# An opening ordered by a list schedule, value's halves swapped and 1/rms by tokens in a linear-attention and SwiGLU kernel

## The chip, the cores and the metric

The kernel runs on one core of a Trainium2 chip. A core has five engines with an instruction queue each: TensorE (PE, with its weight loads as PEld), VectorE (DVE), ScalarE (ACT), GpSimd (POOL) and SyncE (SP, which issues transfers here). The metric is the device time of one execution in microseconds (us), lower is better.

## The reference

The input has 4 batches, 8 heads, 768 steps and 48 dimensions a head. First a linear attention with decay, then a feed-forward block on its output, 3072 tokens of 384 features:

```python
for t in range(S):
    kt, vt, rt = (k[:, :, t], v[:, :, t], r[:, :, t])
    cur = np.einsum('bhd,bhe->bhde', u[None] * kt, vt)
    y[:, :, t] = np.einsum('bhd,bhde->bhe', rt, state + cur)
    state = w[None, :, :, None] * state + np.einsum('bhd,bhe->bhde', kt, vt)
...
rms = np.sqrt(np.mean(x * x, axis=-1, keepdims=True) + 1e-06)
xn = x / rms * rms_g
g = xn @ w_gate
silu = g * (1.0 / (1.0 + np.exp(-g)))
val = xn @ w_val
return (silu * val @ w_out).astype(np.float32)
```

The three feed-forward weights (384 x 1536 twice, 1536 x 384) arrive as 64-bit floats, the rest as 32-bit floats.

## The kernel before

The 768 steps are cut into 12 chunks of 64; a chunk holds all 4 batches, so 256 tokens. Everything is done in 32-bit floats; a product in the code is two passes on TensorE.

**Mixing a chunk.** `mix(s, what)` (line 501) gives a chunk's steps in the order of a string of letters. R and K multiply r and k by powers of the decay (`decay_r`, `decay_k`; tiles ME, MO and CH, the profile's `chan`). 1, 2 and 3 form the bonus u·r·k by tokens (TOK, du), and d writes it as a diagonal into ME and MO (`diagonal`, line 316: on VectorE for chunk 0 and in part for chunk 1, else eight small ScalarE instructions a call and side). a are the scores, 32 small matmuls a half (`pa`), and m copies them under a mask into ME and MO. y are the outputs, 48 matmuls a half (`py`), whose squares (sq) and copies scaled by rms_g (yT) ScalarE keeps. q adds the squares of the three feature blocks on VectorE, r sums them over features with a matrix of ones on TensorE (`pm`, every row the same) and takes the root, n takes the reciprocal of 128 x 256 elements and scales: xa from the upper 64 rows of yT, xb from the lower 64, each copied to the other 64 rows by ScalarE. h weights the keys (KH), u makes the states (`pu`), which ScalarE copies into VS for the next chunk. The next chunk's transfers are issued by the step that frees their tile.

**The feed-forward block.** `gate_val(s, nn)` makes gate and value of 128 features for a chunk, 6 matmuls with xa and the half wa of the weights, 6 with xb and wb; the two halves of the array's rows hold gate and value. A Silu on ScalarE and a product on VectorE give h. `add_cell(q, s)` multiplies three h with a quarter of w_out (`po`) and adds to the chunk's sum.

**Weights.** Each of the 24 pieces of 128 x 576 64-bit floats is loaded by SP into a raw tile and rounded to 32 bits by `round_piece` (line 189): one instruction on ScalarE (ulp), two on VectorE (bits), one sum on POOL (line 209). `rounded(count)` forces rounding up to what a product needs.

**Opening and blocks.** The first two chunks take the plain path in the *opening*, lines 526 to 559 and 673 to 677: calls of `gate_val`, `add_cell`, `mix`, `rounding` and `warm` in an order written out by hand. The opening has 24 `gate_val`, 8 `add_cell` and the mixing of chunks 0 to 3. `warm(n)` gives n matmuls of ones that keep TensorE at work. From line 679 on, the *blocks* treat two chunks at a time, with seven products in place of eight for each pair of feature groups (sums of weights s1 to s4, sums of tokens t1 to t4); they mix the two chunks after them in the same time. Each engine runs in program order: `InOrder` (line 81, recorded as line 89) fixes that for PE, DVE and ACT.

Of the kernel before, what the change touches and what calls it, by code (L numbers as in the profile page):

```python
# [89 lines left out]

@with_exitstack
def fast(ctx, tc, chan, tok, vpad, w, u, wka, wkb, wot, g_cols, out, bad):
# [8 lines left out]
    pe, dve, act = (InOrder(tc, engine) for engine in (nc.tensor, nc.vector, nc.scalar))  # L102
    wide = wka.dtype == I64
    PIECE = NQ * CC * P
    CUT = PIECE // 2
# [11 lines left out]
    raws = loading.enter_context(tc.tile_pool(name="raws", bufs=6))  # L117
# [5 lines left out]
    wraw = c_tile([P, HP], "wraw")  # L123
    dve.memset(wraw, 1.0)
    eps = c_tile([P, 1], "eps")
    dve.memset(eps, EPS)
    w_v = w.rearrange("(a e) d -> e d a", e=2)
    with nc.allow_non_contiguous_dma(reason="w, one column for each pair of heads"):
        for z in range(2):
            act.dma_start(out=wraw[64 * z : 64 * z + D, :], in_=w_v[z])  # L130
# [8 lines left out]
    def load_chan(s):  # L139
        for z in range(2):  # L140
            nc.sync.dma_start(out=CH[64 * z : 64 * z + D], in_=chan[s, z])

    def load_tok(s):
        nc.sync.dma_start(out=TOK, in_=tok[s])

    def load_v(s):
        nc.sync.dma_start(out=VS[64:128, 0], in_=vpad[s, 64:128])
        nc.sync.dma_start(out=VS[0:64, 1], in_=vpad[s, 0:64])

    utab = c_tile([P, HP, D], "utab")  # L150
    gcol = c_tile([P, CC], "gcol")
    for z in range(2):

        (dve, nc.gpsimd)[z].memset(CH[64 * z + 32 : 64 * z + 64], 0.0)
    load_tok(0)
    load_chan(0)
    for z in range(2):
        src = bass.AP(tensor=u.tensor, offset=u.offset + z * D, ap=[[0, 64], [2 * D, HP], [1, D]])
        act.dma_start(out=utab[64 - 64 * z : 128 - 64 * z], in_=src)
    act.dma_start(out=gcol, in_=g_cols)  # L160

    spare = c_tile([P, 1], "spare")
# [6 lines left out]
    pieces = [
        (dst[i], src[i], k) for i in range(WQ) for dst, src in ((wa, wka), (wb, wkb), (wo, wot)) for k in range(2)  # L170
    ]
    PER_Q = len(pieces) // WQ
    queue, staged, state = deque(pieces), deque(), {"done": 0}

    def stage():
        if not queue:
            return
        dst, src, k = queue.popleft()
        cols = slice(k * CUT, (k + 1) * CUT)
        flat = dst.rearrange("p a b -> p (a b)")[:, cols]  # L180
        if not wide:
            nc.sync.dma_start(out=flat, in_=src[:, cols])
            staged.append((flat, None))
            return
        raw = raws.tile([P, CUT], I64, name=f"raw_{len(queue)}", tag="raw")
        nc.sync.dma_start(out=raw, in_=src[:, cols])
        staged.append((flat, raw))

    def round_piece():

        if not staged:
            return
        dst, raw = staged.popleft()
        if raw is not None:
            words = raw.bitcast(I32).rearrange("p (n z) -> p n z", z=2)
            hi, lo = words[:, :, 1], words[:, :, 0].bitcast(U32)
            n = state["done"]
            bits = raws.tile([P, CUT], I32, name=f"bits_{n}", tag="bits", bufs=2)  # L200
            ulp = raws.tile([P, CUT], I32, name=f"ulp_{n}", tag="ulp", bufs=2)
            act.activation(ulp, lo, AF.Copy, scale=2.0**-29)
            dve.tensor_scalar(
                out=bits, in0=hi, scalar1=3, scalar2=0x3FFFFFF8, op0=ALU.logical_shift_left, op1=ALU.bitwise_and
            )
            dve.scalar_tensor_tensor(
                out=bits, in0=hi, scalar=-0x40000000, in1=bits, op0=ALU.bitwise_and, op1=ALU.bitwise_or
            )
            nc.gpsimd.tensor_tensor(out=dst.bitcast(I32), in0=bits, in1=ulp, op=ALU.add)  # L209
        state["done"] += 1  # L210
        stage()

    def rounded(count):
        while state["done"] < count:
            round_piece()

    load_v(0)
    for _ in range(6):
        stage()


    ident = c_tile([P, P], "ident")
    make_identity(nc, ident)
    ones = c_tile([P, P], "ones")
    nc.gpsimd.memset(ones, 1.0)

    nc.gpsimd.memset(KH[32:64, 0], 0.0)
    nc.gpsimd.memset(KH[96:128, 1], 0.0)
    wcol = c_tile([P, HP], "wcol")
    dve.tensor_scalar(out=wcol, in0=wraw, scalar1=W_LOW, scalar2=W_HIGH, op0=ALU.max, op1=ALU.min)  # L230

    dmask, mask = c_tile([P, L], "dmask"), c_tile([P, L], "mask")
    nc.gpsimd.memset(mask, 1.0)
    for z in range(2):
        rows = slice(64 * z, 64 * z + 64)
        nc.gpsimd.affine_select(
            out=mask[rows], in_=mask[rows], compare_op=ALU.is_ge, fill=0.0, base=-1, pattern=[[1, L]],
            channel_multiplier=-1,
        )
    mask_i = mask.bitcast(I32)  # L240
    nc.gpsimd.memset(VS[0:64, 0], 0.0)
    nc.gpsimd.memset(VS[64:128, 1], 0.0)


    pw = raws.tile([P, HP, L], FP32, name="pw", tag="pw", bufs=1)
    dve.memset(pw[:, :, 0:1], 1.0)
    wn, n, pows = wcol, 1, {1: wcol}
    while n < L:
        dve.tensor_mul(pw[:, :, n : 2 * n], pw[:, :, 0:n], free_dims(wn, (1, HP), (0, n)))
        sq = c_tile([P, HP], f"w_{2 * n}")  # L250
        dve.tensor_mul(sq, wn, wn)
        wn, n = sq, 2 * n
        pows[n] = wn
    winv = c_tile([P, HP], "winv")
    dve.reciprocal(winv, pows[L // 2])
    by_inv = free_dims(winv, (1, HP), (0, L))
    up, down = c_tile([P, HP, L], "up"), c_tile([P, HP, L], "down")
    pw_rev = free_dims(pw[:, :, L - 1 :], (L, HP), (-1, L))
    dve.tensor_mul(up, pw, by_inv)
    dve.tensor_mul(down, pw_rev, by_inv)  # L260
    gdup = raws.tile([P, HP, 2, L], FP32, name="gdup", tag="gdup", bufs=1)
    wk = c_tile([P, HP, D], "wk")

    dve.tensor_add(dmask, ident[:, 0:64], ident[:, 64:128])
    for z in range(2):
        dve.tensor_mul(gdup[:, :, z, :], pw_rev, free_dims(pows[L // 2], (1, HP), (0, L)))
    ps = ps_at.tile([P, HP, P], FP32, name="ps_wk", tag="at")
    for p in range(HP):
        pe.transpose(ps[:, p, :], gdup[:, p].rearrange("c z t -> c (z t)"), ident)
    act.copy(wk[64:128], ps[64:128, :, 0:D])  # L270
    act.copy(wk[0:64], ps[0:64, :, 64 : 64 + D])

    for z in range(2):
        rows = slice(64 * z, 64 * z + D)
        for p in range(HP):
# [930 lines left out]
```

## Time and profile before

| | us |
|---|---|
| median of 3 runs (737.05 to 740.19) | 739.49 |
| profiled execution | 739.65 |
| its span, first to last instruction | 737.9 |
| PE busy in the span | 662.3 (90%) |
| PEld, DVE, ACT, POOL busy | 510.7, 402.4, 336.8, 44.7 |
| moved | 61.32 MB, mean 83 GB/s |

PE is the busiest engine; the page's 40 slices show it at nine tenths or more from about the thirteenth slice on and at 4 to 9 tenths before. A share of the whole span says little here, since opening and blocks have different limits: the rows below are cut by stage.

### The profile page before, as it was taken

What the parts mean: (1) busy time and instruction counts of PE and PEld (TensorE: products, weight loads), DVE (VectorE), ACT (ScalarE), POOL (GpSimd) and SP (SyncE); (2) the same over time, 40 slices, a digit from 0 to 9 for tenths busy, and PEclk for the clock granted to TensorE, in tenths of its full rate; (3) what the DMA queues carried; (4) which work ended last, traced back from release to release, by engine and by line L of the source; (5) the groups of instructions that cost most, each with busy time, mean ns of one, the idle gap of its engine ahead of it and who ended that gap; (6) DMA issues with size and microseconds to landing.
All of it is one profiled execution on the core that took longest, in us unless ns stands there. A gap on an engine that the chain in (4) does not pass through costs nothing.

```text
span 737.9 us, 15078 instructions
## 1 busy us (share of the span) xinstructions
PE 662.3 (90%) x6422; PEld 510.7 (69%) x6422; DVE 402.4 (55%) x572; ACT 336.8 (46%) x929; POOL 44.7 (6%) x39
## 2 busy tenths in 40 slices
PE   4668978586879899999999999999999999999992
PEld 4656765364557788668887678886688876788751
DVE  6956635534258775546657257746367662555300
ACT  3454452325322344735646545557356456333331
POOL 3221402112100000000000000000000000000000
PEclk9888998787899999999999999999999999999997
DMA  8835605230222031314143331234230530111132
GB/s 223 270 113 143 206 1 132 74 112 1 60 64 61 1 87 35 75 49 98 33 135 81 98 71 54 89 80 101 73 95 20 147 75 22 39 49 50 49 96 64
DMA packets 20572, 61.32 MB, mean 83 GB/s; under 512 B 3984, under 2 KB 7056, under 8 KB 19344
## 3 DMA queue, kind: packets, MB, share of 16 engines
q1 hardware_dynamic: 19392, 60.17, 30.8%
q8 instruction: 52, 0.85, 0.5%
q10 hardware_dynamic: 1104, 0.10, 0.1%
q14 instruction: 24, 0.20, 0.1%
HBM read 55.54 MB, written 4.72 MB: 82 GB/s over the span
## 4 chain that ended last, share of the span: by engine, by line
PE 77%; DVE 11%; ACT 6%; issue 3%; POOL 1%; DMA 1%; SPq 0%; ACTq 0%; DVEq 0%; POOLq 0%
PE po L89 26%; PE b L89 14%; PE a L89 9%; PE c L89 9%; PE gv L89 7%; PE py L89 4%; PE pa L89 4%; PE pu L89 2%; ACT MO L89 2%; ACT ME L89 2%; PE warm L89 2%; DVE bits L89 2%; DVE h L89 1%; DVE gv L89 1%; DVE ME L89 1%
## 5 line engine op out<-in xcount | busy, mean ns | idle before, releaser
L89 PE MATMUL po<-wo,h 128*128 128x384 f32 x576 | 203.1, 505 | 10.2 <-POOL wo L209 10.2
L89 PEld LDWEIGHTS po<-wo,h 128*128 128x128 f32 x576 | 110.0, 196 | 84.2 <-POOL wo L209 13.0
L89 DVE TENSOR_TENSOR gv<-b,m 128x512 f32<-128x512 f32 x90 | 62.0, 689 | 64.2 <-PE b L89 63.5
L89 ACT ACTIVATE gv<-gv 128x512 f32<-128x512 f32 (+1 forms) x60 | 31.0, 518 | 49.5 <-DVE gv L89 49.5
L89 DVE TENSOR_TENSOR gv<-c,gv 128x512 f32<-128x512 f32 x60 | 41.4, 690 | 16.9 <-PE c L89 15.8
L89 PE MATMUL a<-xa,wa 64*128 64x256 f32 x360 | 45.0, 382 | 1.9 <-DVE h L89 1.9
L89 PE MATMUL b<-xa,wa 64*128 64x256 f32 x360 | 45.3, 384 | 0.6 <-DVE gv L89 0.6
L89 PE MATMUL b<-t,wb 64*128 64x256 f32 x360 | 44.5, 379 | 1.0 <-DVE gv L89 1.0
L89 ACT ACTIVATE ME<-dmask,du 64x64 f32<-64x64 f32 x160 | 39.8, 330 | 12.0 <-DVE du L89 11.6
L89 ACT ACTIVATE MO<-dmask,du 64x64 f32<-64x64 f32 x176 | 44.4, 334 | 0.4
L89 PE MATMUL c<-xb,s 64*128 64x256 f32 x360 | 44.3, 378 | 0.0
L89 PE MATMUL b<-t,s 64*128 64x256 f32 x360 | 44.0, 377 | 0.3 <-DVE gv L89 0.3
L89 PE MATMUL gv<-xa,wa 64*128 64x256 f32 x288 | 42.5, 428 | 1.9 <-POOL wa L209 1.1
L89 PE MATMUL c<-t,s 64*128 64x256 f32 x360 | 43.9, 376 | 0.0
L89 PE MATMUL a<-xb,wb 64*128 64x256 f32 x360 | 43.9, 376 | 0.0
L89 PEld LDWEIGHTS pa<-ME,chan 48*64 48x64 f32 x384 | 26.6, 146 | 23.3 <-issue 16.8
L89 PE MATMUL gv<-xb,wb 64*128 64x256 f32 x288 | 37.4, 391 | 5.7 <-POOL wb L209 5.5
L89 PEld LDWEIGHTS py<-ME,VS 128*64 128x64 f32 (+1 forms) x576 | 34.4, 130 | 10.9 <-issue 10.5
L89 PE MATMUL pa<-ME,chan 48*64 48x64 f32 x384 | 29.9, 234 | 13.2 <-issue 9.4
L89 DVE TENSOR_TENSOR h<-gv,h 128x256 f32<-128x256 f32 x24 | 10.2, 424 | 56.7 <-ACT h L89 56.6
L89 ACT COPY VS<-pu 48x288 f32<-48x288 f32 x88 | 23.2, 312 | 39.1 <-PE pu L89 38.7
L89 PE MATMUL py<-ME,VS 128*64 128x64 f32 (+1 forms) x576 | 37.7, 222 | 2.3 <-DVE MO L89 2.3
(105 smaller groups left out, 1078.0 us busy)
## 6 DMA issues: line engine op xcount, KB each, us to landing
TOK<-in_tok_dram SPq DMA_DIRECT2D x12, 768.0 KB, 4.7
chan<-in_chan_dram SPq DMA_DIRECT2D x24, 384.0 KB, 6.4
VS<-in_vpad_dram SPq DMA_DIRECT2D x24, 336.0 KB, 4.8
raw<-in_wka_dram SPq DMA_DIRECT2D x8, 576.0 KB, 5.7
raw<-in_wkb_dram SPq DMA_DIRECT2D x8, 576.0 KB, 5.1
raw<-in_wot_dram SPq DMA_DIRECT2D x8, 576.0 KB, 3.9
again<-in_wka_dram SPq DMA_DIRECT2D x16, 288.0 KB, 2.8
out_dram<-o SPq DMA_DIRECT2D x48, 96.0 KB, 2.2
```

The source lines that it names most:

```text
L89: return lambda *args, **kwargs: self.tc.keep_in_program_order(give(*args, **kwargs))
```

## The change

The opening's order is made by a program. A class `Plan` records each step as an operation with its engine, an assumed cost, the names that it reads and writes, and the function that gives its instructions. `schedule` is a list schedule: each operation gets a latest start from goals (the products back to back from 25.0 us on), and each engine takes the ready one whose latest start is earliest; DVE and POOL operations marked `port` exclude each other. `run` then gives the instructions in the order of the planned starts, and fills PE's planned idle time before 25 us with matmuls of ones. The blocks keep their order and their strings.

```python
def schedule(self, goals, free):
    ...
    late = [goals.get(i, 1e6 + i) for i in range(n)]
    for i in reversed(range(n)):
        for j in then[i]:
            late[i] = min(late[i], late[j] - self.hop(i, j) - self.ops[i][1])
    ...
    for _ in range(n):
        when, e = min((max(free[e], min(at[i] for i in ready[e])), e) for e in free if ready[e])
        i = min((i for i in ready[e] if at[i] <= when), key=lambda i: late[i])
        sooner = [j for j in ready[e] if at[j] <= when + 0.3 and late[j] < late[i] - 1]
        if sooner:
            i = min(sooner, key=lambda j: late[j])
        s = max(when, at[i])
        if self.ops[i][5]:
            s = max(s, port["POOL" if e == "DVE" else "DVE"])
    ...
    loads(0), quarter(0), mixing(0)
    cell(0, 0)
    loads(1), quarter(1), mixing(1)
    cell(0, 1), cell(1, 0), cell(1, 1)
    loads(2), quarter(2), mixing(2)
    cell(0, 2), cell(1, 2)
    loads(3), quarter(3)
    cell(0, 3)
    mixing(3)
    ...
    p.run(cells, 25.0, {"PE": 1.5, "DVE": 1.5, "ACT": 4.5, "POOL": 6.5, "SP": 1.2}, warm)
```

A `cell(s, i)` is three `gate_val`; its `add_cell` follows the first `gate_val` of the next cell. `gate_val` and `add_cell` share three PSUM banks a, b, c in turn (before: a and b for `gate_val`, c for `add_cell`). The first quarter's gate and value weights come in six pieces of 384 columns, the rest in pieces of 576. Transfers of the opening are operations of SP in the plan, and SP keeps program order too. The first unit sums s4 and s3 of the blocks stand in the opening.

In the mathematics and the data:

```diff
-    both = lambda half: np.stack([gate[:, half], val[:, half]], axis=1)
+    both = lambda half: np.stack([gate[:, half], val[:, 1 - half]], axis=1)
...
-        dve.reciprocal(rms_of[s], rms_of[s])
-        for x, rows, others in ((xa[s], slice(0, 64), slice(64, 128)), (xb[s], slice(64, 128), slice(0, 64))):
-            dve.tensor_mul(x[rows], yT_of[s][rows], free_dims(rms_of[s][rows], (0, CC), (1, NT)))
-            act.copy(x[others], x[rows])
+    def exchange(s, z):
+        act.copy(xb[s][64 - 64 * z : 128 - 64 * z], xa[s][64 * z : 64 * z + 64])
+    def mean_squares(bank, sq):
+        for half in range(2):
+            for i in range(CC):
+                pe.matmul(
+                    bank[:, 2 * P + half : 2 * P + half + 1], sq[:, i, half * P : (half + 1) * P], ones[:, 0:1],
+                    start=i == 0, stop=i == CC - 1, skip_group_check=True,
+                )
+    def root(bank, ms):
+        act.activation(ms, bank[:, 2 * P : 2 * P + 2], AF.Sqrt, scale=1.0 / DM, bias=eps)
+    def inverse(ms, diag):
+        dve.reciprocal(ms, ms)
+        for half in range(2):
+            dve.tensor_scalar_mul(diag[:, half], ident, ms[:, half : half + 1])
+    def spread(bank, diag):
+        pe.matmul(
+            bank[:, 0 : 2 * P], ones, diag.rearrange("p h t -> p (h t)"), start=True, stop=True, skip_group_check=True
+        )
+    def scaled(s, bank, yT):
+        dve.tensor_mul(xa[s], yT, free_dims(bank, (0, CC), (1, NT)))
...
+    def u_k(s, to):
+        for p in range(HP):
+            act.mul(to[:, :, p, :], CH[:, 1, :, p, :], ucol[:, p : p + 1])
+    def diagonal_from(bank, half, side):
+        t, rows = SIDES[side]
+        dve.tensor_mul(
+            t[rows, 2 * half : 2 * half + 2].rearrange("p b h t -> p (b h) t"),
+            bank[rows].rearrange("p (x t) -> p x t", t=L), free_dims(dmask[rows], (0, 2 * HP), (1, L)),
+        )
```

With value's halves swapped, the 128 rows of xa are those of yT scaled, and xb is xa with its halves exchanged. The mean square of the opening's four chunks is taken by tokens (12 passes of one column, `mean_squares`), its root and reciprocal are of 128 x 2 elements, and a matmul of ones with two scaled identities spreads the result over all rows in PSUM (`spread`). The blocks keep squares, root and reciprocal as before and take the single scaling. In chunk 0 the bonus comes from TensorE: u·k on ScalarE, its products with r (32 matmuls a half), and `diagonal_from` cuts the diagonal out of PSUM; in chunks 1 to 3 ScalarE makes all diagonals. Chunk 0's r and k arrive as one tile of 128 rows with zeros included (`chan_0`), so the two memsets of `chan` go; w, u and rms_g arrive as one tile `col`, u by rows as `u_row`.

Where instructions moved, three places. VectorE at the end of chunk 0's mixing, from the weight pieces (bits) to the scaled x (KH are the weighted keys, ms and diag the new reciprocal); before:

```order
L89 TENSOR_TENSOR KH<-TOK,wk 64x768
L89 TENSOR_TENSOR sq_291<-sq_291 128x256 x2
L89 TENSOR_TENSOR KH<-TOK,wk 64x768
L89 TENSOR_SCALAR bits_403<-raw_125 128x576
L89 SCALAR_TENSOR_TENSOR bits_403<-raw_125,bits_403 128x576
L89 TENSOR_SCALAR bits_411<-raw_127 128x576
L89 SCALAR_TENSOR_TENSOR bits_411<-raw_127,bits_411 128x576
L89 RECIPROCAL rms_355<-rms_355 128x256
L89 TENSOR_TENSOR xa_420<-yT_290,rms_355 64x768
L89 TENSOR_TENSOR xb_421<-yT_290,rms_355 64x768
```

and now:

```order
L90 TENSOR_TENSOR KH<-TOK,wk 64x768 x2
L90 RECIPROCAL ms<-ms 128x2
L90 TENSOR_SCALAR diag<-ident,ms 128x128 x2
L90 TENSOR_SCALAR bits_143<-raw_137 128x384
L90 SCALAR_TENSOR_TENSOR bits_143<-raw_137,bits_143 128x384
L90 TENSOR_SCALAR bits_141<-raw_138 128x384
L90 SCALAR_TENSOR_TENSOR bits_141<-raw_138,bits_141 128x384
L90 TENSOR_TENSOR xa_451<-yT_first,at_147 128x768
```

The sums of squares are gone, the reciprocal stands ahead of two pieces that it stood behind, and x is one instruction. Two further pieces stand ahead of KH in both.

TensorE from the mean square of chunk 0 to its third `gate_val` (pu are states, gv products; in the change at_147 and at_148 are the two small PSUM banks, first_a to first_c the three large ones, first_c<-ones the warm-up); before:

```order
L89 MATMUL pm_353<-sq_291,ones 128x256
L89 MATMUL pu_0_359<-VS,KH 48x48 x16
L89 MATMUL pu_1_380<-VS,KH 48x48 x16
L89 MATMUL warm_426<-ones 128x128 x16
L89 MATMUL gv_0_443<-xa_420,wa_107 128x256 x6
L89 MATMUL gv_0_443<-xb_421,wb_111 128x256 x6
L89 MATMUL gv_1_469<-xa_420,wa_107 128x256 x6
```

and now:

```order
L90 MATMUL at_147<-ones,sq_first 128x1 x6
L90 MATMUL first_c<-ones 128x128 x7
L90 MATMUL at_148<-VS,KH 48x48 x16
L90 MATMUL at_147<-diag,ones 128x256
L90 MATMUL first_c<-ones 128x128 x11
L90 MATMUL first_a<-xa_451,wa_123 128x256 x6
L90 MATMUL first_b<-xa_451,wa_123 128x256 x6
L90 MATMUL first_a<-xb_452,wb_127 128x256 x6
L90 MATMUL first_b<-xb_452,wb_127 128x256 x6
L90 MATMUL at_147<-VS,KH 48x48 x16
L90 MATMUL first_c<-xa_451,wa_123 128x256 x6
L90 MATMUL first_c<-xb_452,wb_127 128x256 x6
```

The second half of the states moved behind two `gate_val`, and the halves of these are interleaved, so that wa's products of two come ahead of the first that needs xb.

ScalarE around the second chunk's diagonals (h and hbuf are Silu's results, ulp a weight piece, yT and sq what it keeps of the outputs); before:

```order
L89 ACTIVATE h_1_482<-gv_1_469 128x256
L89 COPY MO<-ME 64x1024
L89 ACTIVATE MO<-dmask,du_485 64x64 x8
L89 ACTIVATE h_2_511<-gv_2_498 128x256
L89 ACTIVATE ulp_516<-raw_131 128x576
L89 ACTIVATE MO<-dmask,du_485 64x64 x8
```

and now:

```order
L90 ACTIVATE hbuf_152<-first_c 128x256
L90 COPY MO<-ME 64x1024
L90 ACTIVATE ulp_145<-raw_139 128x576
L90 ACTIVATE ME<-dmask,du_557 64x64 x8
L90 ACTIVATE MO<-dmask,du_557 64x64 x8
L90 ACTIVATE ME<-dmask,du_557 64x64 x8
L90 ACTIVATE MO<-dmask,du_557 64x64 x8
L90 ACTIVATE yT_first<-at_148,col 128x128 x3
L90 ACTIVATE sq_first<-at_148 128x3x128
L90 ACTIVATE ulp_146<-raw_140 128x576
L90 ACTIVATE hbuf_152<-first_a 128x256
```

All 32 diagonals stand in one run between two Silu; before, 16 of them did, with a Silu between each eight, and VectorE made the other half.

## Rows read from the trace of the kernel before

**Rows 1.** Stages: length, busy us (instructions) by engine, clock, DMA share, GB/s.

```profile
0.00:38.70 38.70, 22.93 (x310) 21.58 (x310) 29.15 (x51) 16.11 (x37) 13.35 (x19) 0.91 0.90 245
38.70:224.50 185.80, 143.20 (x1368) 105.79 (x1366) 92.31 (x126) 73.88 (x189) 31.34 (x21) 0.87 0.32 88
224.50:692.90 468.40, 464.64 (x4654) 365.09 (x4649) 278.49 (x389) 235.58 (x672) 0.00 (x0) 1.00 0.27 69
```

**Rows 2.** TensorE's waits, 38.7 to 224.5: total us, times, longest; eleven rows.

```profile
PE po L89 <- POOL wo L209: 10.2, 3, 6.4
PE pa L89 <- issue: 9.4, 2, 7.2
...
PE py L89 <- DVE MO L89: 0.2, 1, 0.2
```

**Rows 3.** Timeline of TensorE: start, us, instructions; warm-up, products, first block product.

```profile
10.88 6.99 PE L89 MATMUL warm<-ones 128*128 128x128 f32 x40
...
36.78 2.06 PE L89 MATMUL warm<-ones 128*128 128x128 f32 x17
38.77 1.57 PE L89 MATMUL gv<-xa,wa 64*128 64x256 f32 x12
...
77.41 1.46 PE L89 MATMUL gv<-xa,wa 64*128 64x256 f32 x12
...
82.68 4.14 PE L89 MATMUL po<-wo,h 128*128 128x384 f32 x12
86.75 1.57 PE L89 MATMUL gv<-xa,wa 64*128 64x256 f32 x12
...
224.56 1.57 PE L89 MATMUL a<-xa,wa 64*128 64x256 f32 x12
```

**Rows 4.** Busy us of pa, py and pu alone, a half of each at full clock.

```profile
260.00:262.00 2.00, 1.15 (x32) 1.01 (x32) 0.55 (x1) 1.00 0.04 8
274.00:276.20 2.20, 1.59 (x48) 1.44 (x48) 0.10 (x1) 1.00 1.08 179
288.00:289.40 1.40, 0.93 (x32) 0.80 (x32) 0.00 (x0) 1.00 0.00 0
```

**Rows 5.** Timeline of VectorE at the end of the first chunk's mixing.

```profile
27.89 1.97 DVE L89 TENSOR_TENSOR sq<-sq 128x256 f32<-128x256 f32 x2
...
32.96 1.75 DVE L89 RECIPROCAL rms<-rms 128x256 f32<-128x256 f32 x1
34.74 0.95 DVE L89 TENSOR_TENSOR xa<-yT,rms 64x768 f32<-64x768 f32 x1
```

**Rows 6.** Rounding, groups to 224.5 (count, busy us, mean ns, idle), and eight diagonals.

```profile
L89 DVE SCALAR_TENSOR_TENSOR bits<-raw,bits 128x576 int32<-128x576 int32 x24 | 22.5, 939 | 0.8
L89 DVE TENSOR_SCALAR bits<-raw 128x576 int32<-128x576 int32 x24 | 11.2, 466 | 1.7 <-POOL wa L209 1.7
...
L209 POOL TENSOR_TENSOR wo<-bits,ulp 128x576 int32<-128x576 int32 x8 | 13.1, 1638 | 46.5 <-DVE bits L89 42.3 <-ACT ulp L89 4.2
...
L89 ACT ACTIVATE ulp<-raw 128x576 int32<-128x576 uint32 x24 | 17.1, 737 | 0.1
...
52.84 2.01 ACT L89 ACTIVATE MO<-dmask,du 64x64 f32<-64x64 f32 x8
```

**Rows 7.** Timeline of VectorE while POOL sums a piece (43.83 to 45.82).

```profile
43.60 0.95 DVE L89 TENSOR_TENSOR TOK<-TOK 128x768 f32<-128x768 f32 x1
44.58 2.04 DVE L89 TENSOR_TENSOR TOK<-TOK,utab 128x768 f32<-128x768 f32 x1
```

**Rows 8.** Two stretches of loads (last number GB/s), and an issue with us to landing.

```profile
6.00:14.00 8.00, 4.00 (x19) 4.03 (x20) 6.12 (x23) 2.85 (x9) 1.86 (x4) 1.00 1.06 190
16.00:22.00 6.00, 5.09 (x121) 4.86 (x121) 4.74 (x7) 0.48 (x1) 0.00 (x0) 1.00 1.02 410
...
TOK<-in_tok_dram SPq DMA_DIRECT2D x1, 768.0 KB, 4.7
```

**Rows 9.** The stretch after the longest wait of the opening, columns as rows 1.

```profile
50.00:60.00 10.00, 5.98 (x38) 4.04 (x39) 5.52 (x8) 4.83 (x19) 1.84 (x1) 0.50 0.18 60
```

More of the change, by code (lines that the diff above doesn't have):

```diff
@@ L169, in fast @@
[L169 to L187, printed above, removed]
@@ L474, in store @@
             row = (2 * j + bl) * S + s * L
[L475 to L487 removed]
+            sp.dma_start(out=out[row : row + L, :], in_=osb[bl * L : (bl + 1) * L, :])
@@ L488, in add_cell, with give @@
+    def add_cell(s, i, hs):
+        po, keys = next_gv()
+        def give():
+            for j in range(2):
+                for o in range(NQ):
+                    pe.matmul(
+                        po[:, j, 0:DM], hs[o][0][:, j * P : (j + 1) * P], wo[i][:, o, :], start=o == 0, stop=o == NQ - 1
+                    )
+        cells.append(add("PE", 3.87, [h[1] for h in hs] + [f"wo{i}.0", f"wo{i}.1"], keys, give, name=f"P {s} {i}"))
+        if i == 0:
             sums[s] = work.tile([P, 2, DM], FP32, name=f"o_{s}", tag="o", bufs=FIRST)
-            act.copy(sums[s], po[:, :, 0:DM])
+            add("ACT", 0.8, keys, [f"o{s}"], lambda: act.copy(sums[s], po[:, :, 0:DM]), name=f"o {s}")
@@ L570, in fast, with cell @@
-    sum_4 = lambda i: dve.tensor_sub(s4[i], wb[i], s2[i])
+            add("DVE", 0.96, keys, [f"o{s}"], lambda: dve.tensor_add(sums[s], po[:, :, 0:DM], sums[s]), name=f"o {s}")
+        if i == WQ - 1:
+            add("SP", 0.5, [f"o{s}"], [], lambda: [store(sums[s][:, j], s, j) for j in range(2)])
+    def cell(s, i):
+        hs = []
+        for o in range(NQ):
+            hs.append(gate_val(s, i, o))
+            if o == 0 and waiting:
+                add_cell(*waiting.popleft())
+        waiting.append((s, i, hs))
@@ new lines, in fast @@
+    loads(0), quarter(0), mixing(0)
[7 more added lines that the diff above has]
+    mixing(3)
+    add("DVE", 0.2, ["w"], [], w_range)
+    add("DVE", 0.0, ["rounded", "up", "down", "wk"], ["sums"], begin_sums)
+    for n, reads, writes in (
+        (1, ["wa2.0", "wa2.1", "wb2.0", "wb2.1"], ["s1"]), (2, ["s1", "wa0.0", "wa0.1", "wa0.2"], ["s2"]),
+    ):
+        add("DVE", 1.25, ["sums"] + reads, writes, lambda n=n: unit_sum(n, 0), port=True, name=f"sum {n}")
@@ new lines, in fast @@
+    cell(1, 3)
+    for n, reads, writes in (
+        (4, ["s2", "wb0.0", "wb0.1", "wb0.2"], ["s4"]), (3, ["wa0.0", "wa0.1", "wa0.2"], ["wa2.0", "wa2.1"]),
+    ):
+        cells.append(add("DVE", 1.25, ["sums"] + reads, writes, lambda n=n: unit_sum(n, 0), port=True, name=f"sum {n}"))
+    cells.append(add("DVE", 0.95, ["sums", "xa0", "xa2"], ["t1"], lambda: token_sum(2, 1), port=True))
+    cells.append(add("DVE", 0.95, ["t1", "xb0.0", "xb0.1"], ["t2"], lambda: token_sum(2, 2), port=True))
+    while waiting:
+        add_cell(*waiting.popleft())
```

750 lines of the change are left out of this document (457 added, 293 removed).

## The prediction

> **What bounds the kernel now.** I read the sums by stage first, cut at three places: the first product of the first tokens (38.77 us), the first product of the two-chunk blocks (224.56) and the last projections [rows 1, 3]. In the blocks TensorE is busy 464.64 of 468.40 us at full clock: moving work wins nothing there. In the opening, between 38.70 and 224.50, it is busy 143.20 of 185.80 us at a mean clock of 0.87. So this change, which rewrites the opening alone, is worth what the opening holds beyond its matmuls.
>
> The waits of TensorE in the opening come next [rows 2]. There are eleven kinds, from 10.2 us down to 0.2, together the 42.6 us that are missing, and none leads: out weights that POOL has not yet rounded (10.2), scores that wait for a chunk's preparation (9.4, releaser not named), and so on. Each is a step that stands late in its engine's order, not an engine that is full: in that stretch VectorE is busy 92.31 and ScalarE 73.88 of 185.80 us [rows 1]. After such waits the clock falls: between 50 and 60 us it was granted at 0.50, 1.2 of 2.4 GHz, after 7.2 us without a matmul [rows 2, 9].
>
> **What the opening must do.** At full clock two `gate_val` take from 77.41 to 82.68, 2.6 us each, and an `add_cell` from there to 86.75, 4.07 [rows 3]. The opening has 24 and 8: 62.4 + 32.6 = 95 us, before and after. A chunk's mixing is 2 x 1.15 (scores), 2 x 1.59 (outputs) and 2 x 0.93 (states) = 7.3 us with the drains, about 6.9 without [rows 4].
>
> **The change, part by part.**
>
> *The way to the first product.* The first load is now one 128-row transfer of 1.05 MB in place of two of 48 rows behind TOK. While tiles of 48 and 64 rows loaded, 190 GB/s moved, while 128-row weight pieces did, 410; TOK, 0.79 MB, landed 4.7 us after its issue [rows 8]. So chan_0 takes 4.7 + 0.26/0.41 = 5.3 and is there at about 6. ScalarE then makes u times k, while TensorE ends its 26 warm-up matmuls: 52 passes at 6.99/40 = 0.17, at about 10 [rows 3], and the transposes at 11; the products of u k and r (64, as 2 x 1.15) end at 13. VectorE has powers, up, down, R and K done by then. Its four diagonals from PSUM and four masks work on 64 x 512 elements, which I price at 0.7 each (x, of 768, takes 0.95 [rows 5]): 5.6 us, half of the first four under the products, so they end at 17.7, the last outputs at 19.3, their squares at 19.9. The mean square by tokens is new: 12 passes of one column. Passes of 128 columns started (2.06 - 0.28)/16 = 0.11 apart, so at least 1.3 us, and 3.3 if each took the 0.28 of one alone; I take 1.4, since both kinds load the same weights. A reciprocal of two columns and two scaled identities (0.5) replace the RECIPROCAL of 1.75 us [rows 5]. In front of them on VectorE stand two weight pieces (1.6) and the weighted keys (1.9), so it is 22.8, and the spread ends at 23.7. Two more pieces and their sums on POOL come before x (some 2.3). With value's halves swapped x is one product of 128 rows, 0.95 as xa alone was [rows 5]. So the first product starts at **27** instead of 38.77, between 25 and 30. The additions of squares (1.97) and one of two scalings leave VectorE.
>
> Beside a POOL sum a VectorE product of two SBUF tiles took 2.04 us; the one before it took 0.95 [rows 7]. These are the bounds for x, and I take 1.0. The Trainium skill's "SBUF — State Buffer", section "Who interferes with whom", says that a VectorE instruction with at most one SBUF input, outside its two-port modes, does not contend with GpSimd, and x now reads 1/rms from PSUM; by it x is 1.0 in all four chunks. No row here shows this x. At the upper bound four of them add 4 us, if all lie on the path.
>
> *The mixing.* Three further chunks at 6.9 + 1.4 + 0.5 (the spread, about half of a score) = 8.8, and the states of the first chunk, 1.7: **28 us**, 26 to 34 by the bounds of the mean square.
>
> *The order.* Products, mixing, rounding and loads now stand where the list schedule puts them. If TensorE never waited, the opening would be 27 + 95 + 28 = 150 us. Weights, 24 pieces' worth: 0.47 + 0.94 on VectorE (contention included) and up to 1.64 on POOL [rows 6], 34 and 39 us in some 120. Loads: 14.2 MB of weights at 410 GB/s, TOK as fast, the 48- and 64-row tiles at 190 [rows 8], some 75 us in 150. ScalarE: it now makes all diagonals of three chunks, eight in 2.01 [rows 6], 8.0 a chunk, of which VectorE did some; with copies, Silu and rounding some 85 of 120. No engine is full.
>
> *Holes that stay.* I walk the second chunk, whose preparation has only three `gate_val` and half of the states to hide behind. These end at 27 + 7.8 + 0.9 = 35.7. On VectorE, from x at 26: four pieces (4.0), R and K (2.4), three bonus steps (2.8), another piece (1.2), some 2 for POOL's port: 38.5, a hole of 3 before the scores. The diagonals end on ScalarE at about 46 and the masks at 47.5, under a `gate_val`, half the outputs and an `add_cell`: no hole. The reciprocal stands behind five pieces on VectorE: 2 more. Chunks three and four have twelve `gate_val` to hide behind: 2 each. Half clock after the longer holes: 3. Together **12 us**; the ends are 0 and the 42.6 of now.
>
> *Blocks and end.* One scaling less on VectorE in each of eight chunks, 0.95, is off the path: TensorE waited only 3.8 us in all the blocks [rows 1]. Two unit sums of the first block now stand ahead of it, worth 1 of these. The end is untouched.
>
> **The sum.** The blocks start at 27 + 95 + 28 + 12 = 162 instead of 224.56: 62.6 less, and 1 in the first block. The profiled execution took 739.65 us (span 737.9), 0.16 over the median of 739.49, so the forecast is 739.65 - 63.6 = **676 us**. With each part at its best end (25, 26, 0 and all 3.8) it is 657; with 30, 34 and 42.6 it is 717.
>
> **The rivals.**
>
> *ScalarE's diagonals stop the products.* In the second chunk 32 diagonals stand in one run in ScalarE's order, 8.0 us, with the y copies and the next Silu behind them. A product needs one of three banks that Silu empties, so TensorE can run three `gate_val`, 7.8 us, ahead and no more. If each of the three chunks stops TensorE for such a run, that is 24 us: 700. For it: the order. Against it: in the chunks after that, Silu stands between groups of eight. Chance 0.22.
>
> *The clock stays as it is now.* If the 123 us of matmuls ran at today's mean of 0.87 they would take 141: 18 more, 3 of them counted: 691. For it: the stretch after 50 us. Against it: that one follows a wait of 7.2 us, and the blocks use the same three banks at 1.00 throughout [rows 1, 2, 9]. The Trainium skill's "TensorE: Matmul & The Clock Gate", section "A second HAM failure mode: psum-queue depth-cycling", describes a kernel in which small idles between groups that cycle through PSUM banks made the clock swing; by it this rival would be the likely case, and the blocks of this trace don't bear it out. Chance 0.12.
>
> *Slower: the one queue of loads ties everything together.* SP issues in order, and weight loads now stand behind chunk loads that wait for TensorE (chan after the scores, VS after the states), while TensorE waits for weights. Without holes the time is 664; to be slower than now takes 76 us, 2.9 for each of 26 pieces. If TensorE had to wait for the whole rounding of each, 0.47 + 0.94 + 0.74 + 1.64 = 3.8 us [rows 6], that is 99 us: 763. Against it: six raw buffers run ahead, and now the longest kind of wait for POOL is 10.2 us for eight pieces [rows 2]. Chance 0.03.
>
> *It changes nothing.* The orders show that products stand earlier; if loads set the pace all the same, the time would stay at 740. At 88 GB/s in the opening, of 410, nothing supports it [rows 1, 8]. Chance 0.02.
>
> *Better.* No holes, and the first block's waits gone: 660. Chance 0.05.
>
> **How the numbers follow.** The forecast has 0.56, with 664 to 690 as its own range. The range goes from 661 to 703: it leaves out the better case, the last two rivals and a third of the first. A measurement of this kernel can tell 0.5%, 3.7 us, from no change; all but two cases are faster by far more: faster 0.95, same 0.02, slower 0.03.
>
> **What would show it.** In the profile after, the first product should start near 27 us and the first block product near 162, with some 12 us of waits between them in place of 42.6 and a granted clock above 0.93; the blocks should last what they do now, within 4 us. Waits of products for Silu's banks above 15 us would be the first rival, a clock under 0.9 with few waits the second, waits for POOL above 60 us the third. The forecast is wrong if the first product starts after 33, if the opening's waits exceed 30 us, or if the blocks grow.

## The result and the profile after

| | before | changed |
|---|---|---|
| median, us | 739.3 | 675.41 (675.05 to 676.28, 4 runs) |
| span of the profiled execution, us | 737.9 | 673.3 |
| PE busy in it, us | 662.3 (90%) | 649.6 (96%) |
| ratio to before, 95% interval | | 0.9142, 0.9119 to 0.9164 |

The forecast was 676 and the range 661 to 703. Of the runs below, one execution, of the kernel without the bonus on TensorE, was slow (697.86 us at a granted clock of 0.937, the others at 0.987 to 0.989) and is left out. The stages of the profile after, cut at the first product, the first block product and the last projections, in the columns of [rows 1]:

```profile
0.00:27.30 27.30, 25.80 (x382) 24.84 (x382) 20.65 (x49) 15.00 (x38) 9.87 (x17) 1.00 0.94 285
27.30:161.50 134.20, 127.94 (x1420) 99.63 (x1418) 96.54 (x127) 81.92 (x215) 34.51 (x23) 0.97 0.51 141
161.50:628.10 466.60, 463.83 (x4645) 364.81 (x4646) 268.28 (x378) 234.15 (x667) 0.00 (x0) 1.00 0.27 68
```

The span is 64.6 us shorter: 11.4 before the first product (27.3 for 38.7), 51.6 between it and the first block product (134.2 for 185.8), 1.8 in the blocks (466.6 for 468.4), and the end is 0.2 longer (45.2 for 45.0). Of the 51.6, 15.3 are busy time of TensorE (127.94 for 143.20, nearly the same work at a mean clock of 0.97 for 0.87) and 36.3 idle time (6.3 for 42.6). The waits of TensorE in that stretch, to be held against the eleven kinds of [rows 2]:

```profile
PE at L90 <- DVE chan L90: 5.4, 1, 5.4
PE at L90 <- ACT VS L90: 0.5, 1, 0.5
PE at L90 <- DVE diag L90: 0.3, 1, 0.3
PE at L90 <- DVE xa L90: 0.2, 1, 0.2
```

One hole is left: the second chunk's scores wait from 36.45 to 41.80 for its decayed keys (tile `chan`). The way to the first product and to the blocks, in TensorE's timeline (start, us; compare [rows 3]):

```profile
20.32 1.40 PE L90 MATMUL at<-ones,sq_first 128*128 128x1 f32 x12
...
24.80 2.62 PE L90 MATMUL first_c<-ones 128*128 128x128 f32 x22
27.35 1.57 PE L90 MATMUL first_a<-xa,wa 64*128 64x256 f32 x12
...
57.88 1.50 PE L90 MATMUL at<-ones,sq_first 128*128 128x1 f32 x12
...
63.72 0.67 PE L90 MATMUL at<-diag,ones 128*128 128x256 f32 x2 [0.25 <-DVE diag L90]
...
161.55 1.57 PE L90 MATMUL a<-xa,wa 64*128 64x256 f32 x12
```

And VectorE in the hole:

```profile
31.87 2.18 DVE L90 TENSOR_TENSOR TOK<-TOK 128x768 f32<-128x768 f32 x1
33.96 0.75 DVE L90 SCALAR_TENSOR_TENSOR bits<-raw,bits 128x576 int32<-128x576 int32 x1
34.63 1.21 DVE L90 TENSOR_TENSOR ME<-chan,up 128x1024 f32<-128x1024 f32 x1
35.77 2.17 DVE L90 TENSOR_TENSOR TOK<-TOK,utab 128x768 f32<-128x768 f32 x1
...
39.02 0.95 DVE L90 TENSOR_REDUCE du<-TOK 128x16 f32<-128x768 f32 x1
39.88 1.86 DVE L90 TENSOR_TENSOR chan<-chan,down 128x1024 f32<-128x1024 f32 x1
```

VectorE has no gap there; it is simply doing other steps first, and three of them take longer because POOL sums pieces beside them: the two bonus products (TOK) 2.2 us, for 0.95 alone, and the decayed keys 1.86, for 1.21 as the same product of r above. POOL's sums in the same time:

```profile
31.72 1.51 POOL L90 TENSOR_TENSOR wo<-bits,ulp 128x576 int32<-128x576 int32 x1 [0.76 <-DVE bits L90]
34.85 2.27 POOL L90 TENSOR_TENSOR wo<-bits,ulp 128x576 int32<-128x576 int32 x1 [1.63 <-ACT VS L90]
39.25 1.42 POOL L90 TENSOR_TENSOR wa<-bits,ulp 128x576 int32<-128x576 int32 x1 [2.13 <-DVE bits L90]
```

### The profile page after: what moved, and what is told of

Same layout as the page of the kernel before. It is cut to its first block, busy times and chain, and to the rows that moved or that the text cites. A ratio compares the mean times of both kernels' runs of the same rounds, so it can differ in the third digit from the quotient of the medians.

```text
span 673.3 us, 15350 instructions
## 1 busy us (share of the span) xinstructions
PE 649.6 (96%) x6546; PEld 507.8 (75%) x6546; DVE 388.0 (58%) x560; ACT 342.5 (51%) x952; POOL 44.4 (7%) x39
## 4 chain that ended last, share of the span: by engine, by line
PE 82%; DVE 8%; ACT 6%; DMA 2%; issue 2%; SPq 0%; DVEq 0%; ACTq 0%
PE po L90 24%; PE b L90 15%; PE a L90 10%; PE c L90 10%; PE first_c L90 4%; PE first_b L90 4%; PE py L90 4%; PE first_a L90 3%; PE at L90 3%; PE pa L90 3%; ACT MO L90 2%; PE pu L90 2%; DVE bits L90 2%; ACT ME L90 1%; DVE TOK L90 1%
## 5 line engine op out<-in xcount | busy, mean ns | idle before, releaser
L90 PE MATMUL po<-wo,h 128*128 128x384 f32 x480 | 162.5, 491 | 0.0
L90 PEld LDWEIGHTS po<-wo,h 128*128 128x128 f32 x480 | 89.2, 190 | 57.4 <-issue 0.3
L90 PEld LDWEIGHTS a<-xa,wa 64*128 64x128 f32 x360 | 33.8, 187 | 8.8 <-DVE h L90 4.1
L90 PEld LDWEIGHTS b<-t,s 64*128 64x128 f32 x360 | 34.8, 187 | 4.7 <-DVE gv L90 0.7
L90 PEld LDWEIGHTS a<-xb,wb 64*128 64x128 f32 x360 | 34.8, 187 | 4.0
L90 PEld LDWEIGHTS c<-t,s 64*128 64x128 f32 x360 | 34.8, 187 | 4.0
L90 PEld LDWEIGHTS b<-t,wb 64*128 64x128 f32 x360 | 34.4, 187 | 4.4 <-DVE gv L90 0.3
L90 PEld LDWEIGHTS b<-xa,wa 64*128 64x128 f32 x360 | 33.4, 187 | 5.7 <-DVE gv L90 1.5
L90 PEld LDWEIGHTS c<-xb,s 64*128 64x128 f32 x360 | 34.5, 187 | 4.0
L90 ACT ACTIVATE gv<-a 128x256 f32<-128x256 f32 x30 | 11.4, 381 | 48.7 <-PE a L90 48.6
```

Of the source, the lines that this page charges most:

```text
L90: return lambda *args, **kwargs: self.tc.keep_in_program_order(give(*args, **kwargs))
```

## The experiments

Each kernel was timed beside the kernel before. "Against the changed kernel" below is the difference of the two ratios to before, times 739.5 us. An edit to the opening's operations makes the schedule plan anew, so neighbours move as well. The first product also varies by itself: in the changed kernel and in the three runs below with the same order ahead of it (40 and 20 matmuls of ones in the hole, diagonals made twice) it stands at 27.35, 28.70, 27.62 and 27.81 us, so less than 1.4 us in one profile says little.

### The mathematics without the order

In the kernel before, its order by hand kept (mean squares, scaled identities and the spread as in the change):

```diff
-        for x, rows, others in ((xa[s], slice(0, 64), slice(64, 128)), (xb[s], slice(64, 128), slice(0, 64))):
-            dve.tensor_mul(x[rows], yT_of[s][rows], free_dims(rms_of[s][rows], (0, CC), (1, NT)))
-            act.copy(x[others], x[rows])
+        dve.tensor_mul(xa[s], yT_of[s], free_dims(by, (0, CC), (1, NT)))
+        for z in range(2):
+            act.copy(xb[s][64 - 64 * z : 128 - 64 * z], xa[s][64 * z : 64 * z + 64])
```

> The kernel before, its order by hand kept, with value's halves swapped (one scaling of 128 rows in all twelve chunks) and 1/rms by tokens in the opening's four chunks. Theory (the gain is the order's): VectorE is spared some 4.4 us a chunk in the opening (1.97 of sums, 1.75 less 0.6 of reciprocal, 0.95 of scaling), TensorE pays 1.4 + 0.5 a chunk; only where the chain stands in front of products does it count, at the first chunk and perhaps one more: 3 to 8 us less, 731 to 736. Rival (the gain is the mathematics'): the preparation of all four chunks is the path, 4.4 us and the half clock behind it fall each time: under 715. First product 35 to 37 in place of 38.77.

Measured: 733.05 us, ratio 0.9923 (0.9899 to 0.9947). 5.7 us of the 64. The first product starts at 37.32, and its timeline shows why not earlier:

```profile
33.65 3.73 PE L89 MATMUL warm<-ones 128*128 128x128 f32 x32
33.85 0.95 DVE L89 TENSOR_TENSOR xa<-yT,spread 128x768 f32<-128x768 f32 x1 [0.85 <-PE spread L89]
...
37.32 0.49 PE L89 MATMUL gv<-xa,wa 64*128 64x256 f32 x2
```

x is ready at 34.80, but 32 warm-up passes stand ahead of the product in the order by hand: 2.5 us that the shorter chain saved go into matmuls of ones. The first block product comes 6.5 earlier (218.06). The theory holds: in this order, the rest of the gain is not in these operations.

### The operations without the schedule

```diff
-        for i in sorted(range(len(self.ops)), key=lambda i: (self.start[i], i)):
-            ...
-            self.ops[i][3]()
+        idle(9.0)
+        for op in self.ops:
+            op[3]()
```

> The changed kernel with the same operations given in the order in which they are recorded, not in that of the planned starts. Theory (the schedule makes the gain): a chunk's whole mixing then stands on TensorE between products, and its chain (bonus, 8 us of diagonals, masks, outputs, mean square, spread, copies: some 25 us of which TensorE works 9) lies open three times: 3 x 16 = 48 more, with half clock some 60: 720 to 750, TensorE's waits in the opening above 45 us. Rival (the operations themselves make it): within 10 us of the changed kernel, under 686.

Measured: 790.13 us, ratio 1.0689 (1.0661 to 1.0716), slower than the kernel before by 51 and beyond the range given. Its opening, as a window and as waits:

```profile
49.55:267.35 217.80, 150.96 (x1388) 119.85 (x1386) 94.38 (x118) 79.88 (x211) 28.47 (x18) 0.74 0.24 78
```

```profile
PE at L90 <- DVE chan L90: 25.7, 2, 19.6
PE at L90 <- ACT MO L90: 19.7, 1, 19.7
PE at L90 <- DVE KH L90: 7.8, 6, 2.0
```

Two holes of 20 us, one of 6 and a mean clock of 0.74, much as expected. What I had left out is the first chunk: the first quarter's eight pieces are recorded ahead of its mixing, so u·k stands behind eight pieces on ScalarE (24.10 in place of 6.45) and the first product comes at 49.59. The recorded order is one that nobody would choose; what it shows is that the new operations by themselves do not make the gain. Taken back one at a time with the schedule kept, as in the next four runs, they are worth -2.1, 0, 3.7 and 3.8 us of the 64, so nearly all of it is where the steps stand. Three parts were not tested alone: the three PSUM banks in turn, the smaller first pieces and the two unit sums that moved ahead of the blocks.

### 1/rms by features again

```diff
-        add("PE", 1.35, ["sq0", "sq1"], [key], lambda bank=bank: mean_squares(bank, sq), name=f"r {s}")
-        ...
-        add("PE", 0.45, ["diag"], [key], lambda bank=bank: spread(bank, diag), name=f"spread {s}")
+        add("DVE", 1.97, ["sq1"], ["sq0"], add_squares, port=True, name=f"q {s}")
+        add("PE", 0.45, ["sq0"], [key], lambda bank=bank: sum_squares(bank), name=f"r {s}")
+        add("ACT", 0.45 if s == 0 else 3.05, [key], ["rms"], lambda bank=bank: roots(bank), name=f"sqrt {s}")
+        add("DVE", 1.75, [], ["rms"], lambda: dve.reciprocal(rms, rms), name=f"inv {s}")
```

> The changed kernel with the opening's 1/rms by features as in the blocks: squares added on VectorE (1.97), one sum over features, root and reciprocal of 128 x 256 (1.75), no spread; the schedule plans anew. Theory (my term): the first product comes 2.5 to 4 us later (1.97 + 1.75 more, 1.4 + 0.5 + 0.6 less, plus POOL's port), the other three chunks hide it: 676 to 680. Rival: VectorE's time counts in all four chunks: 3 us each, 685 or more. Rival: the hole ahead of the second chunk's scores takes up the delay of the first product: 674 to 676.

Measured: 673.12 us, ratio 0.9114 (0.9095 to 0.9133), 2.1 *less* than the changed kernel; the intervals overlap, the profile says the same:

```profile
29.70 1.57 PE L90 MATMUL first_a<-xa,wa 64*128 64x256 f32 x12
...
59.33 0.59 PE L90 MATMUL at<-sq_first,ones 128*128 128x256 f32 x2
...
159.26 1.57 PE L90 MATMUL a<-xa,wa 64*128 64x256 f32 x12
```

```profile
29.70:159.20 129.50, 122.67 (x1351) 94.98 (x1350) 99.20 (x126) 80.75 (x210) 32.39 (x23) 0.96 0.52 141
```

The first product is 2.35 later, a little less than my term, and the blocks start 2.3 earlier. By tokens a chunk takes 1.50 and 0.67 of TensorE, by features 0.59. Between the two points TensorE is busy 122.67 us for 127.94 and idle 6.8 for 6.3 (the hole ahead of the second chunk's scores is 4.5), so what is gained is TensorE's work and not the hole: three chunks' mean squares make 4.7 of it, and half of the first chunk's states, which here stands ahead of the first product, 0.9. None of the three theories had a gain.

### Two scalings

```diff
-        dve.tensor_mul(xa[s], yT, free_dims(bank, (0, CC), (1, NT)))
+        for z in sides:
+            rows = slice(64 * z, 64 * z + 64)
+            dve.tensor_mul((xa, xb)[z][s][rows], yT[rows], free_dims(bank[rows], (0, CC), (1, NT)))
```

> The changed kernel with value's halves not swapped: two scalings of 64 rows (0.95 each) and a copy behind each, in all twelve chunks. Theory: the first product waits for one copy more (0.83) and, where VectorE sets the second chunk's scores, 1 us; the other chunks and the blocks hide the rest: 675 to 678. Rival: VectorE's 0.95 counts in each of twelve chunks: 685 or more.

Measured: 675.60 us, ratio 0.9143 (0.9120 to 0.9165): no difference. The first product starts at 27.02 and the blocks at 161.73, for 27.35 and 161.55. Scaling x once is worth nothing that can be measured here.

### The bonus of the first chunk on VectorE and ScalarE

```diff
-        quick = s == 0
+        quick = False
```

> The changed kernel with the first chunk's bonus made as in the other chunks (three steps on VectorE, 32 diagonals on ScalarE) and not as products of u k and r on TensorE; the schedule plans anew. Theory: the diagonals' 8 us and 2.9 us of bonus now stand in the first chunk's chain, the first product comes 5 to 7 us later than 27.35; the hole ahead of the second chunk's scores takes up part of that (in the plan all but 1.6), since VectorE has more time for them: 677 to 682. Rival: the opening is a sum in which each us before the first product counts in full: 681 or more with a first product at 33. Rival: the route through TensorE is worth nothing: 675.

Measured: 678.94 us, ratio 0.9192 (0.9162 to 0.9222), 3.7 more.

```profile
32.91 1.12 PE L90 MATMUL at<-diag,ones 128*128 128x256 f32 x2 [2.28 <-DVE diag L90]
35.16 2.93 PE L90 MATMUL first_a<-xa,wa 64*128 64x256 f32 x12 [1.14 <-DVE xa L90]
```

The first product is 7.8 later, more than expected, and at half clock (granted 0.52 from 35.1 to 40.0); half of it comes back: the blocks start at 165.10, 3.55 later. By then the second chunk's keys are ready (45.84, when the products ahead of its scores end at 46.5), and no hole stands before its scores. Here a microsecond before the first product is worth only what the next hole doesn't absorb.

### One load or two

```diff
-        if s == 0:
-            sp.dma_start(out=CH, in_=chan_0)
-            return
...
+    for z in range(2):
+        (dve, pool)[z].memset(CH[64 * z + 32 : 64 * z + 64], 0.0)
```

> The changed kernel with r and k of the first chunk loaded as before the change, in two transfers of 48 rows with two memsets of zeros, not as one of 128 rows. Theory (my term: 190 against 410 GB/s): they land 2 to 3 us later than at 6.2, u k and the scores follow, the first product comes 1 to 3 us later than 27.35, and the hole ahead of the second chunk's scores takes up half: 676 to 677. Rival (the powers of the decay, which wait for another transfer, set the start): 675. Rival (all counts): 678 or more.

Measured: 679.94 us, ratio 0.9194 (0.9169 to 0.9219), 3.8 more, with the first product at 33.60. I had priced the transfer and forgotten the zeros: the load waits for the memset and is issued late.

```profile
1.59 1.76 DVE L90 MEMSET chan<- 32x2048 f32 x1 [0.47 <-issue]
...
10.83 0.69 DVE L90 TENSOR_TENSOR ME<-chan,up 128x512 f32<-128x512 f32 x1 [4.42 <-DMA chan<-in_chan_dram]
```

The issue is at 3.38 for 0.81, the landing 7.4 us after it for 5.4: 2.0 for the transfer, as the term said, and 2.6 for the memset. That is 4.6 of the 6.25 by which the first product is late. VectorE's masks end only 3.1 later (21.13 for 18.06); the rest is TensorE, whose granted clock was 0.50 from 15.0 to 22.5 where the changed kernel had 1.00: 12 passes of ones ahead of the first outputs took 2.93 us for 1.60 and ended at 22.48, after the masks. What made the clock fall there was not tested. The blocks start 3.9 later (165.45), so 2.35 came back, 1.0 of it from the hole ahead of the second chunk's scores (4.4 for 5.4).

### Filling the hole

Does the wait before the second chunk's scores make the half clock behind it, and does that count? Matmuls of ones went ahead of the scores, 40 and then 20:

```diff
+    def warm_in(bank, s, half):
+        if (s, half) == (1, 0):
+            for _ in range(20):
+                pe.matmul(bank[:, 0:P], ones, ones, start=True, stop=True, skip_group_check=True)
```

> The changed kernel with 40 matmuls of ones (some 4.8 us at full clock) on TensorE ahead of the second chunk's scores, in the 5.4 us in which it waited for the decayed keys; nothing else moved. Theory (the wait makes the half clock behind it): the granted clock stays at 1.00 through the stretch from 40.7 to 47.5 in which it was 0.50, the scores, products and outputs there take 3 us less, and as TensorE is the bound there: 672 (671 to 673.5). Rival (what is behind the hole is set by other engines, ScalarE's run of 8 us of diagonals first): the clock is up and the time the same, 675.

Measured: 676.52 us, ratio 0.9155 (0.9135 to 0.9176), 1.0 more, and the clock at 1.00 throughout from the first product to the blocks. This looks like the rival, but the edit was too large:

```profile
37.73 9.20 PE L90 MATMUL at<-ones 128*128 128x128 f32 x80
46.85 0.27 PE L90 MATMUL at<-ME,chan 48*64 48x64 f32 x1
```

A 32-bit matmul is two passes in the trace; 80 passes outlast the hole. Of the 5.05 us by which the scores are late, 1.35 stand before the first product (28.70). Hence half as many:

> The run with matmuls in the hole, with 20 in place of 40: a matmul of ones is two passes in the trace, 40 were 80 passes and 9.2 us, and pushed the second chunk's scores from 41.80 to 46.85; 20 are 4.6 us and end before the keys are there. Theory (the wait makes the half clock, and TensorE sets what is behind it): the scores start at 41.8 to 43, no stretch at 0.50, 3 us less than the changed kernel: 672 (671 to 673.5). In the run before, scores 5.0 late moved the first block product by 1.9 only, which is the same 3.1. Rival: what is behind the hole waits for ScalarE and VectorE anyway: 675.

Measured: 671.95 us, ratio 0.9079 (0.9063 to 0.9094), 4.7 less by ratio and 3.5 by the medians. The stretch 40.7 to 47.5, first of the changed kernel, then of this one:

```profile
40.70:47.50 6.80, 5.70 (x74) 5.24 (x76) 5.97 (x11) 6.72 (x28) 1.42 (x1) 0.50 0.78 245
```

```profile
40.70:47.50 6.80, 6.23 (x118) 5.42 (x118) 6.30 (x11) 6.72 (x29) 1.53 (x2) 1.00 0.88 268
```

From the first product to the first block product:

```profile
27.60:158.70 131.10, 129.99 (x1459) 101.89 (x1458) 96.39 (x127) 81.76 (x215) 34.33 (x22) 1.00 0.52 144
```

That is 131.1 for 134.2: 3.1 us, with no matmul of the kernel moved. The theory holds: beside its own 5.4 us, the wait costs 3.1 behind it.

### The first rival, provoked

Each diagonal of the second chunk made twice; the order stays.

```diff
-                act.mul(t[rows, b, p, :], dmask[rows], du_of[s][rows, x : x + 1])
+                for _ in range(2 if s == 1 else 1):
+                    act.mul(t[rows, b, p, :], dmask[rows], du_of[s][rows, x : x + 1])
```

> The changed kernel, its order unchanged, with each of the second chunk's 32 diagonals made twice on ScalarE: the run from 40.06 to 48.16 lasts 16 us, to 56.2. First rival of the prediction (the run stops the products): the 8 us more count nearly in full: 681 to 684, TensorE waiting for Silu's banks. Theory (the run has slack of its own, since the second half's outputs come at 54.87 only and two gate_val's banks are free until then): 3 to 5 us count: 678 to 680, and what TensorE waits for is the second half's masks and outputs, not Silu.

Measured: 684.12 us, ratio 0.9243 (0.9225 to 0.9260), 7.5 more. ScalarE's run, 40.06 to 48.16 in the changed kernel, lasts 20.2 here and not 16:

```profile
39.89 5.00 ACT L90 ACTIVATE ME<-dmask,du 64x64 f32<-64x64 f32 x16 [0.73 <-DVE du L90]
...
55.01 5.06 ACT L90 ACTIVATE MO<-dmask,du 64x64 f32<-64x64 f32 x16
```

```profile
PE at L90 <- DVE MO L90: 4.7, 2, 4.4
PE at L90 <- DVE chan L90: 4.7, 1, 4.7
PE at L90 <- DVE diag L90: 2.0, 1, 2.0
```

The run is 12 longer and TensorE waits 4.7 for it, so it had some 6 to 7 us of slack; in the changed kernel its last mask ended at 49.15, and the outputs that need it started at 54.87, 5.7 later. TensorE waits for masks in MO, which wait for the diagonals, not for Silu's banks: the theory has the mechanism right. But the waits come with half clock again (0.77 from 41.6 to 60.9) and a late reciprocal (2.0), so the total is as high as the rival's. Both theories were written for a run 8 longer, though; of the 12 it became, 7.5 count by the ratios (9.9 between the first product and the blocks in the profile), a share between the two. Two writes to one place also took 0.31 each for 0.25.

### A better order

One goal of the schedule moved, so that the first add_cell comes ahead of the second chunk's keys:

```diff
+        goals[next(i for i in cells if self.ops[i][6] == "P 0 0")] = 27.0
         self.start = self.schedule(goals, free)
```

> The changed kernel with one goal moved: the first add_cell of the first chunk is given the goal 27.0 in the list schedule, so that its pieces of w_out and the products on VectorE that it needs come ahead of the second chunk's keys and it fills the hole ahead of that chunk's scores. Theory (the hole is an order that the goals chose, not work that lacks): the plan's own end is 3.8 us earlier, the wait of 5.4 us is under 3, and the clock stays up (3 more): 668 to 672. Rival (VectorE and POOL are full between 24 and 44 us, whatever the order): the hole comes back behind the add_cell, 674 to 677.

Measured: 670.99 us, ratio 0.9086 (0.9064 to 0.9107), 4.1 less. That is no more than the 20 matmuls of ones gave (0.9079). Then, besides, 1/rms by features in chunks three and four alone (`tokens = s < 2`):

> The kernel of the run before with, besides, 1/rms by features again in the third and fourth chunk (sums of squares and reciprocals on VectorE), and by tokens in the first two. Theory (by tokens costs TensorE some 1.4 us a chunk that are on the path once products run without a hole, and saves VectorE time that is not): 2 to 3 us less than that run, 665 to 670, with 12 matmuls of one column gone from each of two chunks. Rival (the gain of the run by features came from its other order and not from TensorE's matmuls): the same as that run within 1 us.

Measured: **667.68 us**, ratio 0.9050 (0.9022 to 0.9078), 6.8 less than the changed kernel and the lowest of all runs. First product to first block product in the two runs:

```profile
27.35:158.10 130.75, 126.70 (x1452) 97.66 (x1450) 96.20 (x126) 81.35 (x218) 30.60 (x21) 1.00 0.51 144
```

```profile
27.20:153.70 126.50, 123.11 (x1427) 94.68 (x1426) 99.98 (x126) 81.89 (x218) 30.61 (x21) 1.00 0.52 150
```

In both the add_cell fills the hole, and no stretch is at half clock; the second run's lines:

```profile
36.76 4.14 PE L90 MATMUL first_b<-wo,hbuf 128*128 128x384 f32 x12
41.81 1.57 PE L90 MATMUL first_a<-xa,wa 64*128 64x256 f32 x12 [0.92 <-POOL wa L90]
```

With the add_cell in the hole the stretch is 3.5 shorter than the changed kernel's 134.2, and 3.1 of that is the clock, which the matmuls of ones won as well. The wait's own 5.4 us are not won: TensorE still waits 4.0 (6.3 before), now mostly for the scaled identities (1.5), pieces (1.3 in three waits) and a product of Silu (0.6), and the first half of the first chunk's states, which stood ahead of the first product, stands behind it (0.7).

The second run differs from the first only behind 60 us, and the blocks start 4.4 earlier, some 2.1 a chunk. 1.6 of it is the matmuls' own difference (1.50 and 0.67 against 0.59). In the stretch TensorE is busy 3.6 less and idle 0.7 less, so most of it is TensorE's work, against the rival of that run (order, not matmuls); the schedule planned both chunks anew, and I have not traced the rest.

## Why the prediction was right

**The first product at 27.** It came at 27.35. The transfer landed at 6.2 (6 said), the masks ended at 18.06 (17.7), the mean square took 1.40 (1.4), x 0.94 (1.0) with no contention in any chunk:

```profile
L90 DVE TENSOR_TENSOR xa<-yT_first,at x4: 941/954/955, 26.1 to 155.6; 128x768 f32<-128x768 f32 x4
```

By the Trainium skill's "SBUF — State Buffer", section "Who interferes with whom", x does not contend with GpSimd because it reads 1/rms from PSUM. The trace agrees: the first chunk's x ran beside a POOL sum and took 0.94, where the bonus products, of two SBUF tiles, took 2.2:

```profile
26.11 0.94 DVE L90 TENSOR_TENSOR xa<-yT_first,at 128x768 f32<-128x768 f32 x1
```

```profile
26.33 1.01 POOL L90 TENSOR_TENSOR wb<-bits,ulp 128x384 int32<-128x384 int32 x1 [0.56 <-DVE bits L90]
```

The run by features, whose x reads both inputs from SBUF, had 0.96 in all four chunks too, but no POOL sum ran beside any of them.

Between the masks and x the working is worse than its result. By its own terms the scaled identities end at about 22.1 (squares 19.9, mean square 1.4, some 0.3 for the root, 0.5), not 22.8. The two pieces behind them (2.3) need not wait for the spread and end at 24.4, so that the product would start at 25.4. What the trace has is two pieces and the keys ahead of the reciprocal in 5.2 us for the 3.5 said, with POOL sums from 19.07 to 20.08 and from 20.64 to 22.35 beside them:

```profile
19.20 1.30 DVE L90 SCALAR_TENSOR_TENSOR bits<-raw,bits 128x384 int32<-128x384 int32 x1
20.52 2.63 DVE L90 TENSOR_TENSOR KH<-TOK,wk 64x768 f32<-64x768 f32 x2
```

So 27 held some 1.6 us that no term named, and contention beyond what I had priced took as much. That it came within 0.35 is in part luck.

**95 of products and 28 of mixing.** TensorE is busy 127.94, of which some 3 are half clock: 125 for 123.

**12 of holes.** They were 6.3 of waits and 3.1 of clock, 9.4. Near in sum, not in parts. The hole before the second chunk's scores was 5.4 for 3: I walked VectorE to 38.5, and it was done at 41.74. One microsecond of that is x itself, which the walk left out (it begins at 26, where x begins). I also gave POOL's port 2 us in all, and the two bonus products alone lost 1.2 each, the keys 0.7, and weight pieces some 1.6. The reciprocal behind five pieces cost 0.3 for 2, and chunks three and four 0.7 for 4. The half clock was 3.1 for 3, in one stretch. The stage came out at 134.2 for 135 because the 2.6 less in holes and the 1.8 more in products and mixing nearly cancel.

**1 in the blocks.** They lasted 1.8 less, with 2.8 us of waits for 3.8.

**The rivals.** ScalarE's diagonals did not stop the products (no wait for them in the trace after); the run that provoked it shows that the 8.0 us in a row had some 6 to 7 us of slack, and that what TensorE waits for beyond it is masks and not Silu's banks. The price that I wrote, 24 us for three chunks, was not tested. The clock stayed up: one stretch of 6.8 us at 0.50, then 1.00 to the end of the blocks, with the products cycling through three banks. By the Trainium skill's "TensorE: Matmul & The Clock Gate", section "A second HAM failure mode: psum-queue depth-cycling", the rival would have been the likely case; the trace does not bear that out. The one queue of loads tied nothing together: in the trace after TensorE waited neither for POOL nor for a transfer.

**What I priced with the wrong sign.** I wrote the mean square by tokens into the mixing (1.9 a chunk) and its gain into the first product, and never set the one against the other. It helps the first product by 2.35 and costs TensorE more in the three chunks behind, some 2 us net in the runs here. The scaling of x once, the other named part of the mathematics, is worth nothing. The sum held because the order outweighs both.

## What to carry to other kernels

Cut the trace by stage and ask which engine the stage waits for after the change, not before it: the sum moved from VectorE to TensorE brought the first product 2.35 us forward, and cost some 2 us a chunk once the order had made TensorE the bound. A list schedule is as good as its goals and costs: one goal moved here gave 4 us. And a wait on TensorE can cost more than its length: here 3.1 us of half clock stood behind a wait of 5.4, and matmuls of ones won the 3.1 back as well as an add_cell did. So when a hole can't be filled with work, fill it with matmuls of ones counted by the trace's passes, no longer than the hole. Count as won only what the stage gained: work moved into a hole can leave other waits behind it.

## What the hardware showed that I had not expected

A small transfer landed with the large one beside it. The column tile `col`, 5.5 KB, issued at the same time as the 1 MB load, took 5.6 us to land (the large one 5.4) and held back the powers of the decay. In the nine runs with the same two loads it took 5.1 to 6.1, each time 0.2 or 0.3 more than the large one. Where the loads of r and k were issued 2.6 later (section "One load or two"), it took 1.6:

```profile
col<-in_cols_dram ACTq DMA_DIRECT2D x1, 5.5 KB, 5.6
```

```profile
col<-in_cols_dram ACTq DMA_DIRECT2D x1, 5.5 KB, 1.6
```

A scaling of 128 x 128 with one tensor input lost time beside POOL: 1.54 us at most for 0.28 (min, median, max in ns). The second chunk's pair took 1.73 from 61.84 on, while POOL summed a piece from 61.87 to 63.29; the first chunk's, alone, 0.48. By the Trainium skill's "SBUF — State Buffer", section "Who interferes with whom", a `tensor_scalar` can run in a mode that takes the port shared with GpSimd; the row agrees with contention, and no run here shows the mode.

```profile
L90 DVE TENSOR_SCALAR diag<-ident,ms x8: 274/284/1537, 23.3 to 151.6; 128x128 f32<-128x128 f32 x8
```
